# Attention with 192-wide heads beside a gated feed-forward, on one core: the last 64 value channels split by key parity instead of by query halves, and the vector engine's side work placed differently

## The chip, the core and the metric

The kernel runs on one core of a Trainium2 chip. The metric is the device time of one execution in microseconds; runs are compared by their median.

## The reference, cut to what matters

```python
def _A_ref(x, k_cache, v_cache, wq, wo):        # x: 1 x 2048 x 640, caches: 1 x 32 x 2048 x 192
    q = (x @ wq).reshape(B, Sq, H, Dh).transpose(0, 2, 1, 3)
    scores = einsum("bhqd,bhkd->bhqk", q, k_cache) * (Dh ** -0.5)
    p = softmax(scores, axis=-1)
    o = einsum("bhqk,bhkd->bhqd", p, v_cache)
    return o.transpose(0, 2, 1, 3).reshape(B, Sq, H * Dh) @ wo
def _B_ref(x, w1, w3, w2):                      # 640 -> 1536 -> 640
    return (silu(x @ w1) * (x @ w3)) @ w2
xn = layernorm(A_x)
return A_x + _A_ref(xn, ...) * silu(_B_ref(xn, ...))
```

Everything is bf16 in memory. There are 32 heads (H), each with 2048 queries and 2048 keys.

## The kernel before

**Tiling.** The work goes head by head (`h`), in each head by four query blocks of 512 (`qb`), and in each block by eight steps (`p`). A step handles 256 keys: keys lie on 128 partitions, and a second index (`t` or `u`, 0 for even and 1 for odd keys) holds the two keys of a partition. `scores` writes 128 keys x 1024 (even and odd keys, 512 queries each) into one PSUM tile `st2`; `weights` takes the exponential of it on ScalarE into `pT2` (line 558); `values` or `values_quads` multiplies `pT2` by the values `vt` and accumulates over the eight steps into two PSUM tiles, `obank` (`acc["o"]`), of two banks each.

**Quads.** Heads 2 to 30 (`in_quads`) run TensorE as four 64 x 64 arrays. Two of them share an output half (column halves, `c`), two share the rows of the contraction (`r`); the two row halves write to different tiles `acc["o"][0]` and `acc["o"][1]`, which are added at the end. `values_quads` (line 629) has three parts per step: `high(0)` and `high(1)` make the first 128 of 192 channels from even and odd keys, four matmuls of 512 queries each; `low` makes the last 64 channels. Before the change the column halves of `low` hold the two halves of the queries: four matmuls of 256 queries for the even keys and four for the odd keys. Its 256 columns fill half of the second bank of each tile.

**End of a block.** `evict_quads` runs after the last `low` of a block: a ScalarE copy of the first tile to SBUF (`oa`, line 653), a VectorE addition of the second tile (`ot`, line 654), and a DMA transpose into `ox` (line 655). The tiles `obank` are single, so the next block's first `values` matmuls wait for both. All instructions named here are pinned to the order in which the program writes them. `step` writes, at `p == 1` of the next block, first what is left of the old block with `evict_quads`, then the exponential of step 1, and then `project_chunk`: 40 matmuls (line 355) that make the next head's queries, into a tile of the same pool as the scores. That pool (`ps_st`, tag `st2`) has two buffers A and B. Step 0's scores use A, step 1's B, the projection A, step 2's B again. So step 2's scores wait for step 1's exponential, and ScalarE makes that one behind the copy `oa`.

**Row sums.** The sums of the softmax are made on VectorE from `pT2` (`row_sums`): `fours` adds two `pT2` tiles, `join`, `fold` and `ends` (line 662) bring a block to 512 columns, and a DMA transpose turns the result (`eT`, line 688). `turned_sums` reduces it, takes the reciprocal `rl`, and writes the scaled outputs into `ostage` (lines 702 to 709). These steps are put off by a number of steps with `later` and are run by `do_chores` when the step counter has come so far. `pT2` has three buffers, so an exponential three tiles on waits for `fours`. In the last head (`h == H - 1`) `do_chores` does nothing at the first two steps of a block.

**Bound steps.** What the next head needs for its softmax shift (maxima over the keys, column lengths of the query weights, `head_bound`) stands in a list `lazy`; `do_chores` takes one entry at certain steps of a block (`slots`): steps 5, 6 and 7 in even heads and head 1, step 5 in the other odd heads.

After the heads come the rest of the feed-forward and the output projection.

Of the kernel before, what the change touches and what calls it, by code (L numbers as in the profile page):

```python
# [10 lines left out]
ALU = mybir.AluOpType  # L11
AX = mybir.AxisListType
BF16 = mybir.dt.bfloat16
F32 = mybir.dt.float32
I32 = mybir.dt.int32

P = 128
DH = 192
DT = DH - P
# [11 lines left out]
def _kernel_impl(ctx, tc, A_x, A_k_cache, A_v_cache, A_wq, A_wo, B_w1, B_w3, B_w2, out):  # L31
    nc = tc.nc
    _, SQ, D = A_x.shape
    _, H, SK, dh = A_k_cache.shape
# [5 lines left out]
    NQB = SQ // 512  # L40
    NKT = SK // P
    NPAIR = NKT // 2
# [11 lines left out]
    ROWS = (slice(0, DT), slice(DT, P))  # L54
# [21 lines left out]
    pin = tc.keep_in_program_order  # L76
# [73 lines left out]
    def in_quads(h):  # L150
        return 1 < h < H - 1
# [14 lines left out]
    with ExitStack() as actx:  # L166
# [27 lines left out]
        sums = lnx.tile([P, len(ASUM)], F32, name="sums")  # L194
# [122 lines left out]
        acc = {}  # L317
# [245 lines left out]
        def stage(h, qb):  # L563
            if (h // HG, qb) not in stages:
                stages[h // HG, qb] = [stp.tile([P, 4, HG * DH], BF16, tag=f"ostage{qb}", name="ostage"), HG]
            return stages[h // HG, qb][0]

        def staged(h, qb):
            stages[h // HG, qb][1] -= 1
            if stages[h // HG, qb][1] == 0:  # L570
                g0 = h - h % HG
                keep = pin if in_quads(h) else (lambda x: x)
                acc["store"] = keep(nc.sync.dma_start(
                    out=o_scr[qb].rearrange("(t p) c -> p t c", p=P)[:, :, g0 * DH:(g0 + HG) * DH],
                    in_=stages.pop((h // HG, qb))[0][:, :, :]))
# [46 lines left out]
        def values_quads(hd, qb, p, pT2):  # L622
            vt = hd["L"]["vt"]

            def sums(t, low):
                for c in range(2):
                    c0, q0, n = (P, c * 256, 256) if low else (c * DT, 0, 512)
                    for r in range(2):
                        pin(nc.tensor.matmul(acc["o"][r][ROWS[c], int(low), 0:n], lhsT=vt[ROWS[r], t, p, c0:c0 + DT],  # L629
                                             rhs=pT2[ROWS[r], t * 512 + q0:t * 512 + q0 + n],  # L630
                                             start=(p == 0 and t == 0), stop=(p == NPAIR - 1 and t == 1)))

            def high(t):
                if p == 0 and t == 0:
                    acc["o"] = [ps_o.tile([P, 2, 512], F32, tag=f"ob{b}", name=f"obank{b}") for b in range(2)]
                sums(t, False)

            def low():
                sums(0, True)
                sums(1, True)  # L640
                if p == NPAIR - 1:
                    evict_quads(hd, qb, [ob[:].rearrange("p t c -> p (t c)")[:, 0:768] for ob in acc["o"]])

            fs = [lambda: high(0), low, lambda: high(1)]
            if p in (0, NPAIR - 1):
                fs = [fs[0], fs[2], fs[1]]
            return [((hd["h"], qb), f) for f in fs]

        def evict_quads(hd, qb, banks):
            oa = aq["one"].tile([P, 768], F32, tag="oa", name="oa")  # L650
            ot = aq["two"].tile([P, 768], BF16, tag="ot", name="ot")
            ox = aq["two"].tile([P, 6, P], BF16, tag="ox", name="ox")
            pin(nc.scalar.copy(out=oa[:], in_=banks[0]))  # L653
            pin(nc.vector.tensor_tensor(out=ot[:], in0=oa[:], in1=banks[1], op=ALU.add))  # L654
            pin(nc.sync.dma_start_transpose(out=ox[:], in_=ot[:]))
            hd["ox"][qb] = ox

        def later(wait, f, *a):
            chores.append((clock[0] + wait, f, a))

        def add(out, a, b):
            pin(nc.vector.tensor_tensor(out=out, in0=a, in1=b, op=ALU.add))  # L662

        def row_sums(hd, qb, p, w):
            sm = hd["sums"]

            def fours():
                t = aq["tree"].tile([P, 2, 1024], BF16, tag="tree", name="tree")
                a, b = sm["w"]
                sm["w"] = []  # L670
                add(t[:], a[:], b[:])
                sm["t"].append(t)

            def join():
                a, b = sm["t"]
                add(a[:], a[:], b[:])
                sm["t"].pop()

            def fold():
                t = sm["t"][0]  # L680
                add(t[:, 0, :], t[:, 0, :], t[:, 1, :])

            def ends():
                t = sm["t"].pop()[:, 0, :]
                e = aq["two"].tile([P, 512], BF16, tag="e", name="e")
                add(e[:], t[:, 0:512], t[:, 512:1024])
                eT = aq["two"].tile([P, 4, P], BF16, tag="eT", name="eT")
                pin(nc.sync.dma_start_transpose(out=eT[:], in_=e[:]))
                later(6, turned_sums, hd, qb, eT)

            sm["w"].append(w)
            if p % 4 == 3:
                later(2, fours)
            if p == NPAIR - 1:
                for f in (join, fold, ends):
                    later(4, f)

        def turned_sums(hd, qb, eT):
            h, hg = hd["h"], hd["h"] % HG
            ox = hd["ox"].pop(qb)  # L700
            rs = stt.tile([P, 4], F32, tag="rs", name="rs")
            pin(nc.vector.tensor_reduce(out=rs[:], in_=eT[:], axis=AX.X, op=ALU.add))
            rl = rl_all[:, h * NQT + qb * 4:h * NQT + qb * 4 + 4]
            pin(nc.vector.reciprocal(out=rl, in_=rs[:]))
            o0 = hg * DH

            pin(nc.vector.tensor_tensor(out=stage(h, qb)[:, :, o0:o0 + P], in0=ox[:, 0:4, :],
                                        in1=rl.unsqueeze(2).to_broadcast([P, 4, P]), op=ALU.mult))
            pin(nc.vector.tensor_tensor(out=stage(h, qb)[:, :, o0 + P:o0 + DH].rearrange("p (c j) d -> p c j d", c=2),
                                        in0=ox[:, 4:6, :].rearrange("p j (c d) -> p c j d", c=2),  # L710
                                        in1=rl.rearrange("p (c j) -> p c j", c=2).unsqueeze(3).to_broadcast([P, 2, 2, DT]),
                                        op=ALU.mult))
            staged(h, qb)

        clock = [0]
# [2 lines left out]
        aq = {}  # L718

        def do_chores(h, qb, p):  # L720
            if h == H - 1 and p < 2:
                return
            for c in [c for c in chores if c[0] <= clock[0]]:
                chores.remove(c)
                c[1](*c[2])
            slots = (5, 6, 7) if h % 2 == 0 or h == 1 else (5,)
            if p in slots and lazy and lazy[0][0] <= clock[0]:
                _, f, a = lazy.pop(0)
                f(*a)
# [15 lines left out]
        def step(hd, qb, p, extra=None):  # L745
            me = (hd["h"], qb)
            first = qb == 0 and p < 2
            st2 = scores(hd, qb, p, quads=before["quads"] if first else hd["quads"])
            old = [k for k, _ in parts if k != me]
            old_quads = bool(old) and heads_quads(old[0][0])  # L750
            if p == 1 and old_quads:
                while parts[0][0] != me:
                    next_part()
            pT2 = weights(st2, hd["nb"][qb], p)
            parts.extend((values_quads if hd["quads"] else values)(hd, qb, p, pT2))
            if hd["quads"] and p % 2 == 1:
                row_sums(hd, qb, p, acc["w"])
            if p == 0:
                while sum(k != me for k, _ in parts) > (2 if old_quads else 1):
                    next_part()  # L760
            elif p == 1:
                while parts[0][0] != me:
                    next_part()
            else:
                while len(parts) > (4 + (p > 2) if hd["quads"] else 3):
                    next_part()
            if extra:
                extra()
            while late:
                late.pop(0)()  # L770
            clock[0] += 1
            do_chores(hd["h"], qb, p)
# [129 lines left out]
        hx = fw.tile([P, SQ], BF16, name="hx")  # L902
        astack = ExitStack()
        fdp = astack.enter_context(tc.tile_pool(name="fdp", bufs=1, side="right"))
        for name, n in (("one", 1), ("two", 2), ("tree", 3)):
            aq[name] = astack.enter_context(tc.tile_pool(name=f"aq_{name}", bufs=n, side="right"))
        ffn_w_loads = [
            lambda: pin(nc.gpsimd.dma_start(out=w1_sb[:], in_=B_w1[:, FPIG + P:F].rearrange("(c p) f -> p c f", p=P))),
# [57 lines left out]
        for h in range(1, H):  # L966
# [10 lines left out]
            hd = heads[h]  # L977
# [420 lines left out]
```

## Time and profile before

| | us |
|---|---|
| median of 3 runs | 1926.5 (1925.24 to 1927.55) |
| the profiled execution, its own time | 1925.79 |
| its span | 1924.3 |
| TensorE (PE) busy | 1914.5 (99%) |
| VectorE (DVE) busy | 1446.4 (75%) |
| ScalarE (ACT) busy | 1350.4 (70%) |
| GpSimd (POOL) busy | 600.3 (31%) |

The heads end at about 1636 us of the span; the feed-forward and the output projection follow, and there VectorE and ScalarE have little to do. In a profile line, L558 is line 558 of the kernel; "out<-in" names the tiles; "x116" is a count; PEld are weight loads, which run beside the matmuls; SPq is the queue of SyncE, which starts DMAs. In the timeline a row begins with its start and its length in us, and a bracket at its end says how long the engine had been idle before, and what ended that.

### The profile page before, as it was taken

Reading aid. Unit: us, or ns where it says so; the run is one execution under the profiler, and the core shown is the slowest. Engines: PE = TensorE matmul, PEld = TensorE weight load, DVE = VectorE, ACT = ScalarE, POOL = GpSimd, SP = SyncE. Lnnn points to the kernel's source line nnn. Section 1 sums busy time; section 2 is a strip of 40 time slices with the busy share of each in tenths; the row PEclk is TensorE's granted clock in tenths of the full one; section 3 lists DMA queues with packets and bytes.
Section 4 is the critical chain, followed back from the end, with each engine's and each line's share of the span. In section 5 each row is a group of like instructions: output and inputs, shape, how many; then the busy total and the mean of one; then the engine's idle time right before and its main releaser. Section 6 shows DMA issues by size and latency. Waiting matters only on the chain.

```text
span 1924.3 us, 75788 instructions
## 1 busy us (share of the span) xinstructions
PE 1914.5 (99%) x34631; PEld 1306.8 (68%) x34631; DVE 1446.4 (75%) x2326; ACT 1350.4 (70%) x1405; POOL 600.3 (31%) x757
## 2 busy tenths in 40 slices
PE   9999999999999999999999999999999999999999
PEld 5666667777777777777777777777777796454446
DVE  8668888888888888988888888888888875521111
ACT  7778888888888888888888888888888877210000
POOL 3433434343434333344333343433343320000000
PEclk9999999999999999999999999999999999999999
DMA  7714446444553455345544453446444523936763
GB/s 171 142 50 74 106 84 102 86 100 87 93 98 86 99 84 100 81 105 91 101 84 104 76 107 68 112 77 110 77 106 85 97 45 119 281 71 152 162 151 76
DMA packets 535684, 197.22 MB, mean 102 GB/s; under 512 B 486896, under 2 KB 528848, under 8 KB 535360
## 3 DMA queue, kind: packets, MB, share of 16 engines
q1 hardware_dynamic: 522416, 162.71, 43.5%
q0 software_dynamic: 8256, 24.58, 4.9%
q8 instruction: 271, 4.44, 1.0%
q10 hardware_dynamic: 4688, 5.05, 0.8%
q14 instruction: 53, 0.43, 0.1%
HBM read 54.26 MB, written 31.98 MB: 45 GB/s over the span
## 4 chain that ended last, share of the span: by engine, by line
PE 99%; SPq 0%; DVE 0%; ACT 0%; DMA 0%; POOL 0%; issue 0%; ACTq 0%
PE st L550 34%; PE obank L629 31%; PE ps L355 14%; PE ps_s L1142 8%; PE obank L609 3%; PE ps_s L1098 3%; PE ps_f L1162 2%; PE ps_gu L929 1%; PE ps_f L1178 1%; PE ps L340 0%; DMA KT<-in_A_k_cache_dram 0%; SPq L116 0%; PE ps_gu L340 0%; ACT pT L558 0%; SPq L100 0%; ACT xnT L283 0%
## 5 line engine op out<-in xcount | busy, mean ns | idle before, releaser
L558 ACT ACTIVATE pT<-st,nb 128x1024 bf16<-128x1024 f32 x1016 | 1124.6, 1113 | 182.0 <-PE st L550 151.6
L629 PE MATMUL obank<-pT,vt 64*64 64x256 bf16 (+1 forms) x14848 | 787.8, 323 | 0.0
L629 PEld LDWEIGHTS <-vt 64*64 64x64 bf16 x14848 | 499.7, 107 | 172.4 <-issue 1.9
L550 PE MATMUL st<-qS,KM 64*64 64x512 bf16 (+1 forms) x1951 | 416.7, 376 | 0.4 <-POOL qS L381 0.4
L550 PE MATMUL st<-qA,KT 64*64 64x512 bf16 (+1 forms) x1951 | 416.6, 376 | 0.0
L550 PE MATMUL st<-qD,KT 64*64 64x512 bf16 (+1 forms) x1951 | 416.6, 376 | 0.0
L550 PE MATMUL st<-qA,KM 64*64 64x512 bf16 (+1 forms) x1951 | 392.0, 376 | 0.0
L550 PE MATMUL st<-qS,KT 64*64 64x512 bf16 (+1 forms) x1951 | 391.9, 376 | 0.1
L550 PE MATMUL st<-qF,KT 64*64 64x512 bf16 (+1 forms) x1951 | 391.8, 376 | 0.0
L550 PEld LDWEIGHTS <-KT 64*64 64x64 bf16 (+1 forms) x7808 | 286.6, 107 | 129.8 <-issue 0.6
L381 POOL COPY qS<-qA 64x512 bf16<-64x512 bf16 x256 | 291.0, 1137 | 63.9 <-DVE qA L378 28.2
L662 DVE TENSOR_TENSOR tree<-pT,pT 128x2048 bf16<-128x2048 bf16 x232 | 299.7, 1292 | 1.6 <-ACT pT L558 1.6
L355 PE MATMUL ps<-xnT,wq 64*64 64x512 bf16 (+1 forms) x2390 | 291.8, 376 | 0.0
L355 PE MATMUL ps<-xnS,wq 64*64 64x512 bf16 (+1 forms) x2390 | 288.0, 376 | 0.0
L662 DVE TENSOR_TENSOR tree<-tree 128x2048 bf16<-128x2048 bf16 x232 | 265.8, 1146 | 4.0
L355 PEld LDWEIGHTS <-wq 64*64 64x64 bf16 (+1 forms) x4780 | 170.2, 107 | 74.7
L550 PEld LDWEIGHTS <-KM 64*64 64x64 bf16 (+1 forms) x3904 | 152.0, 106 | 54.8 <-issue 1.2
L385 POOL COPY qD<-qF 64x512 bf16<-64x512 bf16 x127 | 95.6, 753 | 292.1 <-ACT qF L378 288.2
L1142 PE MATMUL ps_s<-oT,wo_sb 128*128 128x512 bf16 x720 | 155.7, 379 | 0.0
L378 DVE CAST qA<-ps 128x512 bf16<-128x512 f32 x120 | 82.9, 691 | 95.2 <-ACT qF L378 94.6
L654 DVE TENSOR_TENSOR ot<-oa,obank 128x768 bf16<-128x768 f32 x116 | 110.1, 949 | 36.2 <-ACT oa L653 35.8
L653 ACT COPY oa<-obank 128x768 f32<-128x768 f32 x116 | 92.6, 798 | 62.8 <-PE obank L629 62.8
(159 smaller groups left out, 1628.8 us busy)
## 6 DMA issues: line engine op xcount, KB each, us to landing
o_scr<-ostage SPq DMA_DIRECT2D x64, 384.0 KB, 3.2
vt<-in_A_v_cache_dram SPq DMA_DIRECT2D x62, 384.0 KB, 4.9
wo_sb<-in_A_wo_dram POOLq DMA_DIRECT2D x1, 7680.0 KB, 30.6
wq<-in_A_wq_dram POOLq DMA_DIRECT2D x31, 160.0 KB, 4.2
hT_scr<-hblk SPq DMA_DIRECT2D x16, 256.0 KB, 2.9
xnS<-xnT POOLq DMA_DIRECT2D x8, 320.0 KB, 6.1
wq<-in_B_w_dram POOLq DMA_DIRECT2D x31, 80.0 KB, 3.7
wq<-in_A_wq_dram POOLq DMA_DIRECT2D x31, 80.0 KB, 3.3
```

Of the source, the lines that this page charges most:

```text
L355: pin(nc.tensor.matmul(halves[t][c, :], lhsT=w[ROWS[t], s, c], rhs=xs[ROWS[t], s // 2, qs], start=(s == 0), stop=(s == 2 * DC - 1)))
L378: pin(c(out=dst[:, qs], in_=src))
L381: keep(nc.gpsimd.tensor_copy(out=qS[ROWS[t], qs], in_=qA[ROWS[1 - t], qs]))
L385: keep(copy(out=qD[:, qs], in_=qF[PGW:P, qs]))
L550: pin(nc.tensor.matmul(st2[c, t * 512:(t + 1) * 512], lhsT=k[:, c], rhs=q[ROWS[t], qs], start=(s == 0), stop=(s == 2)))
L558: pin(nc.scalar.activation(out=pT2, in_=st2[:], func=ACT.Exp, scale=SCALE, bias=nb[:]))
L609: pin(nc.tensor.matmul(acc["o"][b][:, r, (j % 2) * 256:(j % 2) * 256 + DH + 1], lhsT=pT2[ROWS[r], t * 512 + j * P:t * 512 + (j + 1) * P], ...
L629: pin(nc.tensor.matmul(acc["o"][r][ROWS[c], int(low), 0:n], lhsT=vt[ROWS[r], t, p, c0:c0 + DT], rhs=pT2[ROWS[r], t * 512 + q0:t * 512 + q0 ...
L653: pin(nc.scalar.copy(out=oa[:], in_=banks[0]))
L654: pin(nc.vector.tensor_tensor(out=ot[:], in0=oa[:], in1=banks[1], op=ALU.add))
L662: pin(nc.vector.tensor_tensor(out=out, in0=a, in1=b, op=ALU.add))
L1142: pin(nc.tensor.matmul(ps_of[d], lhsT=wo_sb[:, k, d * P:(d + 1) * P], rhs=part(k // KQ)[:, k % KQ, :], start=(k == 0), stop=(k == OC - 1)))
```

## The change

The last 64 channels: the column halves of `low` now hold the key parities. Column half 0 takes the even keys and half 1 the odd keys, each for all 512 queries, so `low` is four matmuls of 512 per step in place of eight of 256. The second bank of each tile is filled whole, and `oa`, `ot` and `ox` grow from 768 to 1024 columns. After the transpose the two parities lie beside each other in `ox`; `turned_sums` adds them (64 + 64 columns for each of four query tiles), and then scales.

The side work: the last head no longer skips `do_chores` at the first two steps; the last `turned_sums` of head 30 is put off by 9 steps instead of 6; in even heads the blocks 0 and 2 use the steps 5 and 6 for `lazy`, the blocks 1 and 3 still 5, 6 and 7. The pool of the `tree` tiles has two buffers instead of three.

```diff
             def sums(t, low):
                 for c in range(2):
-                    c0, q0, n = (P, c * 256, 256) if low else (c * DT, 0, 512)
+                    c0, u = (P, c) if low else (c * DT, t)
                     for r in range(2):
-                        pin(nc.tensor.matmul(acc["o"][r][ROWS[c], int(low), 0:n], lhsT=vt[ROWS[r], t, p, c0:c0 + DT],
-                                             rhs=pT2[ROWS[r], t * 512 + q0:t * 512 + q0 + n],
-                                             start=(p == 0 and t == 0), stop=(p == NPAIR - 1 and t == 1)))
+                        pin(nc.tensor.matmul(acc["o"][r][ROWS[c], int(low), :], lhsT=vt[ROWS[r], u, p, c0:c0 + DT],
+                                             rhs=pT2[ROWS[r], u * 512:(u + 1) * 512],
+                                             start=(p == 0 and (low or t == 0)), stop=(p == NPAIR - 1 and (low or t == 1))))
...
             def low():
                 sums(0, True)
-                sums(1, True)
                 if p == NPAIR - 1:
-                    evict_quads(hd, qb, [ob[:].rearrange("p t c -> p (t c)")[:, 0:768] for ob in acc["o"]])
+                    evict_quads(hd, qb, [ob[:].rearrange("p t c -> p (t c)")[:] for ob in acc["o"]])
...
         def evict_quads(hd, qb, banks):
-            oa = aq["one"].tile([P, 768], F32, tag="oa", name="oa")
-            ot = aq["two"].tile([P, 768], BF16, tag="ot", name="ot")
-            ox = aq["two"].tile([P, 6, P], BF16, tag="ox", name="ox")
+            oa = aq["one"].tile([P, 1024], F32, tag="oa", name="oa")
+            ot = aq["two"].tile([P, 1024], BF16, tag="ot", name="ot")
+            ox = aq["two"].tile([P, 8, P], BF16, tag="ox", name="ox")
...
-                later(6, turned_sums, hd, qb, eT)
+                later(6 if in_quads(hd["h"] + 1) or qb < NQB - 1 else 9, turned_sums, hd, qb, eT)
...
-            pin(nc.vector.tensor_tensor(out=stage(h, qb)[:, :, o0 + P:o0 + DH].rearrange("p (c j) d -> p c j d", c=2),
-                                        in0=ox[:, 4:6, :].rearrange("p j (c d) -> p c j d", c=2),
-                                        in1=rl.rearrange("p (c j) -> p c j", c=2).unsqueeze(3).to_broadcast([P, 2, 2, DT]),
-                                        op=ALU.mult))
+            low = ox[:, 4:8, 0:DT]
+            pin(nc.vector.tensor_tensor(out=low, in0=low, in1=ox[:, 4:8, DT:P], op=ALU.add))
+            pin(nc.vector.tensor_tensor(out=stage(h, qb)[:, :, o0 + P:o0 + DH], in0=low,
+                                        in1=rl.unsqueeze(2).to_broadcast([P, 4, DT]), op=ALU.mult))
...
         def do_chores(h, qb, p):
-            if h == H - 1 and p < 2:
-                return
             for c in [c for c in chores if c[0] <= clock[0]]:
                 chores.remove(c)
                 c[1](*c[2])
-            slots = (5, 6, 7) if h % 2 == 0 or h == 1 else (5,)
+            slots = (5,) if h % 2 and h > 1 else (5, 6) if h > 1 and qb % 2 == 0 else (5, 6, 7)
...
-        for name, n in (("one", 1), ("two", 2), ("tree", 3)):
+        for name, n in (("one", 1), ("two", 2), ("tree", 2)):
```

## The prediction, made before the changed kernel was run

> **What bounds the kernel now.** I read the page first (busy times, then the chain that ended last), then the groups kept apart by shape, then the chain and the timeline of one query block.
>
> ```profile
> span 1924.3 us, 75788 instructions
> PE 1914.5 (99%) x34631; PEld 1306.8 (68%) x34631; DVE 1446.4 (75%) x2326; ACT 1350.4 (70%) x1405; POOL 600.3 (31%) x757
> PE 99%; SPq 0%; DVE 0%; ACT 0%; DMA 0%; POOL 0%; issue 0%; ACTq 0%
> ...
> L629 PE MATMUL obank<-pT,vt 64*64 64x512 bf16 x7424 | 608.0, 376 | 0.0
> L629 PE MATMUL obank<-pT,vt 64*64 64x256 bf16 x7424 | 385.7, 269 | 0.0
> L654 DVE TENSOR_TENSOR ot<-oa,obank 128x768 bf16<-128x768 f32 x116 | 110.1, 949 | 36.2 <-ACT oa L653 35.8
> L653 ACT COPY oa<-obank 128x768 f32<-128x768 f32 x116 | 92.6, 798 | 62.8 <-PE obank L629 62.8
> L558 ACT ACTIVATE pT<-st,nb 128x1024 bf16<-128x1024 f32 x1016 | 1124.6, 1113 | 182.0 <-PE st L550 151.6 <-DVE km L466 4.2 <-DVE tree L662 3.7
> ```
>
> TensorE carries the whole chain and is hardly ever idle. So only two things count: what the change saves TensorE, and every wait that it puts in front of TensorE, in full, since TensorE has no slack to catch up with. There are 116 quad blocks (the count of `oa`), with eight steps each, 928 steps.
>
> **TensorE's own work.** The chain of one block in order of time:
>
> ```profile
> 803.39 0.43 PE obank L629 x12
> 803.82 2.16 PE ps L355 x40
> 805.98 0.65 PE st L550 x12
> ...
> 809.44 0.65 PE obank L629 x16
> 810.09 0.65 PE st L550 x12
> ```
>
> A step of values has 16 matmuls before: eight of 512 columns and eight of 256. It takes 0.65 us, as long as the 12 score matmuls of 512. Spread over four arrays, both stream 3 x 512 columns, so eight matmuls of 256 cost what four of 512 cost, within the 0.01 us of the row. A finer bound comes from the block. By the next part's windows it repeats every 12.54 us, and it holds 48 + 10 = 58 groups of four matmuls of 512 (or two of 256); the projection shows 2.16 / 10 = 0.216 us for a group. 58 x 0.216 = 12.53, which leaves 0.01 us for eight `low` parts, 1 to 3 ns each with the rounding. I take 2 ns x 928 = **-2 us** (from 0 to -4.6, the 0.005 us by which the rows can be off).
>
> The Trainium skill ("TensorE: Matmul & The Clock Gate", "Wait — 56ns, not 53.3ns?") states a fixed cost of about 2.5 ns per warm matmul. With one matmul fewer on each array per step that gives -2.3 us, an estimate from the page; the trace agrees as far as it resolves.
>
> **The wider copy, and what stands behind it.** The start of a block, from the timeline, the windows of five blocks and one place where step 2's scores did wait:
>
> ```profile
> 803.86 0.80 ACT L653 COPY oa<-obank 128x768 f32<-128x768 f32 x1 [0.55 <-PE obank L629]
> 804.56 1.12 ACT L558 ACTIVATE pT<-st,nb 128x1024 bf16<-128x1024 f32 x1
> 805.78 0.38 PE L550 MATMUL st<-qS,KM 64*64 64x512 bf16 x1
> 805.81 0.38 PE L550 MATMUL st<-qA,KM 64*64 64x512 bf16 x1
> ...
> 1544.92 1.12 ACT L558 ACTIVATE pT<-st,nb 128x1024 bf16<-128x1024 f32 x1
> 1546.09 0.37 PE L550 MATMUL st<-qS,KM 64*64 64x512 bf16 x1
> ...
> 841.70:854.24 12.54, 12.54 (x269) 9.06 (x265) 11.59 (x24) 10.19 (x10) 3.11 (x3) 1.00 0.53 123
> 879.44:891.98 12.54, 12.54 (x269) 9.07 (x265) 11.92 (x17) 10.50 (x11) 3.28 (x4) 1.00 0.27 29
> ...
> L378 ACT CAST qF<-ps 128x512 bf16<-128x512 f32 x123 | 72.0, 586 | 41.9 <-PE ps L355 41.9
> ```
>
> ScalarE is 70% busy, but not at this place. The copy `oa` starts when the old block's last `low` is done (803.86). Step 1's exponential stands behind it in program order and ends at 804.56 + 1.12 = 805.68. Step 2's scores need its PSUM buffer, and TensorE, coming out of the projection, is there at 805.78. At 1546 the first array was early and really waited: 1544.92 + 1.12 = 1546.04 to 1546.09, so the release takes 0.05 us. The cover is therefore 0.05 us on the first array, and 0.08 on the other three, which come at 805.81.
>
> The copy grows by 256 columns. From 512 to 768 columns ScalarE's copies go from 586 to 798 ns, 0.83 ns per column, so +0.21 us. The exponential then ends at 805.89, TensorE is released at 805.94, and the three later arrays lose 805.94 - 805.81 = 0.13 us (the first loses 0.16, of which 0.03 only uses up its lead). The projection cannot cover more: it is already done. The end of the last `low` is no earlier either, since the same columns are streamed. Of 116 blocks the last runs its step 2 in head 31, where this was not the last wait; 115 x 0.13 = **+15 us**. Bounds: 0.10 per block if the release is a little faster (+11.5); 0.23 if the copy of 1024 took as long as the exponential of 1024, 1113 ns (+26).
>
> **VectorE.** `ot` grows too: from the cast of 512 f32 columns (691 ns, below) to 768 (949) it is 1.0 ns per column, +0.26 us. `turned_sums` gets one addition of 128x256, and its last multiplication keeps its size.
>
> ```profile
> L378 DVE CAST qA<-ps 128x512 bf16<-128x512 f32 x120 | 82.9, 691 | 95.2 <-ACT qF L378 94.6
> L709 DVE TENSOR_TENSOR ostage<-ox,rl_all 128x256 bf16<-128x256 bf16 x116 | 48.4, 418 | 0.0
> 810.50 0.43 DVE L662 TENSOR_TENSOR e<-tree 128x512 bf16<-128x512 bf16 x1
> ...
> 778.95 1.22 DVE L662 TENSOR_TENSOR tree<-pT,pT 128x2048 bf16<-128x2048 bf16 x1
> 780.09 0.95 DVE L654 TENSOR_TENSOR ot<-oa,obank 128x768 bf16<-128x768 f32 x1
> 781.35 0.41 PE L629 MATMUL obank<-pT,vt 64*64 64x512 bf16 x4
> ```
>
> The addition is not in the trace. Between half of the 0.43 of a 512-wide addition and the 0.42 of the same size, with about 0.1 us more because the multiplication now depends on it, it is 0.3 to 0.45 us. Queued behind it are `fours` and then `ot`, and TensorE's next values wait for `ot`. In most blocks `ot` waits for `oa` (idle before it: 35.8 us over the group) and ends 0.7 us or more before TensorE needs it, so 0.21 + 0.26 fit. Not so where the queue is full. At block 3 of an even head (head 14 above, where steps 5, 6 and 7 still hold bound work) `ot` ends at 781.04. Then +0.56 to +0.71 and 0.05 for the release give 781.65 to 781.80, against 781.38 for the second tile's matmuls plus the 0.13 above, 781.51. That is 0.15 to 0.3 us in 14 even heads, **+3 us**. Blocks 0 of even heads, as full before, lose a key maximum at step 7 and gain room. It goes to block 1 with its two GpSimd copies, the column lengths follow one place later, and the head's bound with its GpSimd reduction moves one place on in block 2; the next head needs that five or more steps later, so I cost these moves at nothing, and at one late exponential per even head if the cover fails. None of them carries a DMA with it. Range 0 to +9 (0.6 us per even head, one more block late in each).
>
> The DMA transpose of `ox` carries a third more; its data are used a block later, so I cost it at nothing. If that cover failed, a late transpose would push `turned_sums`, `fours` and `ot` by its lateness. The `tree` tiles with two buffers cost nothing: writers and readers are all on VectorE, in order.
>
> **The last head.** Around 1586 us TensorE has its one long wait among the heads:
>
> ```profile
> ACT pT L558 <- DVE tree L662: 3.7, 1, 3.7
> PE obank L609 <- ACT pT L558: 2.9, 1, 2.9
> 1582.67 0.95 DVE L654 TENSOR_TENSOR ot<-oa,obank 128x768 bf16<-128x768 f32 x1 [5.86 <-ACT oa L653]
> 1585.21 0.68 DVE L702 TENSOR_REDUCE rs<-eT 128x4 f32<-128x512 bf16 x1
> 1587.08 1.22 DVE L662 TENSOR_TENSOR tree<-pT,pT 128x2048 bf16<-128x2048 bf16 x1
> 1588.41 2.12 ACT L558 ACTIVATE pT<-st,nb 128x1024 bf16<-128x1024 f32 x2 [3.73 <-DVE tree L662]
> ```
>
> The exponential needs a `pT` buffer that `fours` still reads, and `fours` waits at step 2 because the last head skips its chores. VectorE was idle for 5.86 us just before. Without the skip, `rs` to `fours` run in that hole and the wait goes: **-2.9 us**. What is late next is the scores themselves, which TensorE paces. If `rs` waits for its DMA there, 1 us may come back. Head 30's last `turned_sums`, put off by three steps, writes only into `ostage`; its store goes out with head 31, so nothing waits for it.
>
> **Sum.** -2 + 15 + 3 - 2.9 = +13.1 us on the profiled execution's own 1925.79 (span 1924.3 and 1.5 around it), 1938.9. The median of the runs lies 0.7 higher, 1926.5, so I predict **1939.6 us**. A difference within 0.2% (3.9 us) is about what a measurement of this kernel cannot tell from none.
>
> **The rivals.**
> *The exponential's end stays hidden* (ends not slower). Place: step 2's scores of each block. It decides at a growth of 0.05 to 0.08 us of the copy: if the copy grew no more, only -2 - 2.9 + 3 remain, 1924.6. Against it: 586 to 798 ns for 256 columns, and the same 12.54 us in blocks 38 us apart, so the cover has no room elsewhere. 0.07.
> *A matmul has a large fixed cost* (ends faster). If each of the 256-wide matmuls carried some 25 ns that a wider one would not repeat, one fewer per array and step is 928 x 25 = 23 us: 1939.6 + 2 - 23 = 1918.6. Against it: the equal 0.65 us of 16 and 12 matmuls above. The Trainium skill ("TensorEngine Tiling (Array Packing)", "Instruction Overhead") speaks of about 60 cycles for each matmul, which would be this case; the trace does not show it at 256 columns. 0.03.
> *VectorE becomes the bound.* The fuller of the two windows above has VectorE busy for 11.92 of 12.54 us; with 0.26 + 0.4 it would be 12.58. If `ot` comes 0.2 us late in half of all blocks, 58 x 0.2 = 11.6 us instead of 3: 1948; more with slower additions, 1955. For it: the full blocks; against: the window before has 11.59, and most have idle time before `ot`. 0.10.
>
> **How the numbers follow.** The forecast has the remaining 0.80; its terms at their ends give 11.5 - 4.6 - 2.9 + 0 = +4 and 26 - 0 - 1.9 + 9 = +33. All terms at their upper ends together are unlikely; I take +4 to +27, 1930 to 1953, which also holds the lower part of the VectorE case. Slower by over 0.2%: 0.80 and 0.10, less 0.04 for a forecast whose terms all come out low, 0.86. Within 0.2%: the hidden case less a little that falls lower, and that 0.04, 0.08. Faster: 0.06.
>
> **What would show it.** Right: `oa` near 1.01 us; step 2's scores starting 0.05 us after the exponential behind `oa`; a block period of about 12.65 us (12.54 + 0.13 - 0.02); the line-609 wait of 2.9 us gone; `ot` late only after block 3 of even heads. Wrong: a block period still at 12.54 or below, or values steps below 0.64 us, or `ot` late in many blocks.

## The result, and the profile after

The changed kernel takes 1939.27 us (median of 6 runs, 1939.19 to 1940.69), the kernel before 1927.2 us (6 runs, 1925.24 to 1927.98). The ratio is 1.0066, with a 95% interval of 1.0056 to 1.0076: slower by 0.7%, a small loss, but clear of the spread of the runs. The span of the profiled execution grew from 1924.3 to 1937.6 us.

The page of the changed kernel:

```profile
span 1937.6 us, 68457 instructions
PE 1929.3 (100%) x30896; PEld 1266.1 (65%) x30919; DVE 1510.7 (78%) x2442; ACT 1375.1 (71%) x1405; POOL 592.1 (31%) x757
PE 97%; DVE 1%; DMA 1%; SPq 0%; ACT 0%; issue 0%; POOL 0%
```

and its groups by shape:

```profile
L629 PE MATMUL obank<-pT,vt 64*64 64x512 bf16 x11136 | 794.2, 376 | 0.3 <-DVE ot L653 0.2
L653 DVE TENSOR_TENSOR ot<-oa,obank 128x1024 bf16<-128x1024 f32 x116 | 141.3, 1218 | 36.4 <-ACT oa L652 35.6
L652 ACT COPY oa<-obank 128x1024 f32<-128x1024 f32 x116 | 117.4, 1012 | 62.2 <-PE obank L629 62.2
L709 DVE TENSOR_TENSOR ox<-ox 128x256 bf16<-128x256 bf16 x116 | 32.9, 283 | 0.0
```

TensorE has 3712 matmuls fewer: its weight loads went from 34631 to 30919, and 23 of the matmuls are missing from this trace. It is still the chain, but now VectorE and a DMA hold 1% of it each. The copy takes 1012 ns instead of 798, the addition 1218 instead of 949, and there is a new addition of 283 ns.

A page that says "PE 100% busy" hides the loss: a matmul's row lasts 0.38 us, but the next group of four starts 0.22 us behind it, so rows overlap and a late one only starts late. It is seen in the chain of one block in order of time (start, length, what):

```profile
811.00 2.16 PE ps L355 x40
813.16 0.80 PE st L550 x12
813.96 1.08 PE obank L629 x20
815.04 0.65 PE st L550 x12
```

The 12 score matmuls behind the projection take 0.80 us, where they took 0.65 in the kernel before; the next 12, at 815.04, take 0.65 again. The timeline shows why (start, length, engine, line, operation):

```profile
811.04 1.01 ACT L652 COPY oa<-obank 128x1024 f32<-128x1024 f32 x1 [0.54 <-PE obank L629]
811.95 1.12 ACT L558 ACTIVATE pT<-st,nb 128x1024 bf16<-128x1024 f32 x1
...
813.12 0.37 PE L550 MATMUL st<-qS,KM 64*64 64x512 bf16 x1
813.12 0.40 PE L550 MATMUL st<-qA,KM 64*64 64x512 bf16 x1
813.13 0.40 PE L550 MATMUL st<-qS,KM 64*64 64x512 bf16 x1
813.13 0.40 PE L550 MATMUL st<-qA,KM 64*64 64x512 bf16 x1
813.33 0.37 PE L550 MATMUL st<-qA,KT 64*64 64x512 bf16 x1
813.36 0.38 PE L550 MATMUL st<-qS,KT 64*64 64x512 bf16 x1
```

The exponential ends at 811.95 + 1.12 = 813.07, and the scores start 0.05 us later. Groups of four matmuls are 0.216 us apart; this one starts 0.372 us after the last group of the projection.

At the last head, the view of waits between 1592 and 1620 us, where the wait of 2.9 us would now be:

```profile
ACT pT L558 <- PE st L550: 3.8, 9, 1.0
DVE osum L581 <- PE obank L609: 3.0, 1, 3.0
DVE rs L701 <- DMA eT<-e: 2.4, 1, 2.4
```

No TensorE wait is left there, and the exponential no longer waits for VectorE.

**Where the 13.3 us are.** Read from the trace as the time from one projection's first matmul to the next, the median block takes 12.672 us, before 12.538. With 115 blocks that is +15.4 us. Blocks over the median cost 1.2 us more than before, the stretch from the last quad block to the feed-forward fell from 51.73 to 48.64 us (-3.1), and the feed-forward and output projection are the same (286.65 us from the start of their first to that of their last matmul in both).

The term of the last head rests on one profile of the kernel before, and its time, 1925.79 us, lies below the median of 1927.2. The five other profiled kernels that keep the skip (among the runs below) spend 53.2 to 53.6 us in this stretch. With 53.3 in place of 51.73 the term is -4.7, and the sum +11.9, which is what lies between the two medians (12.1).

### The profile page after: what moved, and what is told of

It reads as the page before. It is cut to its first block, busy times and chain, and to the rows that moved or that the text cites. A ratio compares the mean times of both kernels' runs of the same rounds, so it can differ in the third digit from the quotient of the medians.

```text
span 1937.6 us, 68457 instructions
## 1 busy us (share of the span) xinstructions
PE 1929.3 (100%) x30896; PEld 1266.1 (65%) x30919; DVE 1510.7 (78%) x2442; ACT 1375.1 (71%) x1405; POOL 592.1 (31%) x757
## 4 chain that ended last, share of the span: by engine, by line
PE 97%; DVE 1%; DMA 1%; SPq 0%; ACT 0%; issue 0%; POOL 0%
PE st L550 34%; PE obank L629 31%; PE ps L355 14%; PE ps_s L1139 8%; PE obank L609 3%; PE ps_s L1095 3%; PE ps_f L1159 2%; PE ps_gu L926 1%; PE ps_f L1175 1%; DMA eT<-e 0%; DVE tree L661 0%; PE ps L340 0%; DMA KT<-in_A_k_cache_dram 0%; SPq L116 0%; DVE ot L653 0%
## 5 line engine op out<-in xcount | busy, mean ns | idle before, releaser
L629 PE MATMUL obank<-pT,vt 64*64 64x512 bf16 x11136 | 794.2, 376 | 0.3 <-DVE ot L653 0.2
L629 PEld LDWEIGHTS <-vt 64*64 64x64 bf16 x11136 | 430.7, 107 | 193.1 <-issue 3.7
L550 PE MATMUL st<-qS,KM 64*64 64x512 bf16 (+1 forms) x1951 | 423.8, 377 | 0.3 <-POOL qS L381 0.3
L550 PE MATMUL st<-qD,KT 64*64 64x512 bf16 (+1 forms) x1951 | 424.0, 376 | 0.0
L550 PE MATMUL st<-qA,KT 64*64 64x512 bf16 (+1 forms) x1951 | 423.9, 376 | 0.0
L550 PEld LDWEIGHTS <-KT 64*64 64x64 bf16 (+1 forms) x7808 | 297.1, 106 | 128.3 <-issue 0.6
L355 PEld LDWEIGHTS <-wq 64*64 64x64 bf16 (+1 forms) x4780 | 182.5, 107 | 83.2
L653 DVE TENSOR_TENSOR ot<-oa,obank 128x1024 bf16<-128x1024 f32 x116 | 141.3, 1218 | 36.4 <-ACT oa L652 35.6
L652 ACT COPY oa<-obank 128x1024 f32<-128x1024 f32 x116 | 117.4, 1012 | 62.2 <-PE obank L629 62.2
L1139 PEld LDWEIGHTS <-wo_sb 128*128 128x128 bf16 x720 | 70.4, 98 | 84.9 <-issue 0.2
```

What stands on the lines that cost most here:

```text
L355: pin(nc.tensor.matmul(halves[t][c, :], lhsT=w[ROWS[t], s, c], rhs=xs[ROWS[t], s // 2, qs], start=(s == 0), stop=(s == 2 * DC - 1)))
L550: pin(nc.tensor.matmul(st2[c, t * 512:(t + 1) * 512], lhsT=k[:, c], rhs=q[ROWS[t], qs], start=(s == 0), stop=(s == 2)))
L629: pin(nc.tensor.matmul(acc["o"][r][ROWS[c], int(low), :], lhsT=vt[ROWS[r], u, p, c0:c0 + DT], rhs=pT2[ROWS[r], u * 512:(u + 1) * 512], sta ...
L1139: pin(nc.tensor.matmul(ps_of[d], lhsT=wo_sb[:, k, d * P:(d + 1) * P], rhs=part(k // KQ)[:, k % KQ, :], start=(k == 0), stop=(k == OC - 1)))
```

## The experiments

The theory: ScalarE's wider copy holds up the exponential, and that holds up TensorE. The rivals: VectorE's added work, or the matmuls themselves. Ratios are against the kernel before, run on the same chip.

**The matmuls alone.** The four 512-wide matmuls, with the old eviction of 768 columns; the last 64 channels of this kernel's output are therefore incomplete.

```diff
# in the kernel before
-                    c0, q0, n = (P, c * 256, 256) if low else (c * DT, 0, 512)
+                    c0, u = (P, c) if low else (c * DT, t)
...
                 sums(0, True)
-                sums(1, True)
```

> The kernel before with the changed matmuls alone: four of 512 columns in the low part, while the copy, the addition and the transpose still take 768 columns. The odd keys' share of the last 64 channels is left out of the output. If the loss sits in the wider copy, this kernel has none of it and gains only what eight matmuls of 256 cost more than four of 512: 2 us, so about 0.999 of the kernel before. If a matmul carried a large fixed cost, some 25 ns on each array and step, it would be 23 us faster (0.988). If the new matmuls themselves cost the 13 us, it is as slow as the changed kernel (1.007).

Measured: 1925.57 us, ratio 0.9993 (0.9984 to 1.0002). The interval reaches 1, so the gain is not shown by the times; the trace resolves it. The median block takes 12.518 us, 0.020 less than before, 2.3 us over 115 blocks. (It is 12.538 or 12.539 in all four profiles with the old matmuls and no added delay.) A `low` part is 2 to 3 ns shorter. The 23 us of a large fixed cost and a loss in the matmuls are both excluded. That the span shrank only by 0.3 us comes from the last head, whose stretch (53.34 us) was 1.6 us longer than in the profile before, as in the other kernels that keep the skip; its reason was not followed.

**A delay behind the copy, in three sizes.** One more ScalarE instruction between `oa` and the exponential, everything else as before, but for the `tree` pool, which has two buffers as in the changed kernel. The first try read `oa` itself:

```diff
             pin(nc.scalar.copy(out=oa[:], in_=banks[0]))
+            oj = aq["one"].tile([P, 185], BF16, tag="oj", name="oj")
+            pin(nc.scalar.copy(out=oj[:], in_=oa[:, 0:185]))
```

> The kernel before with one more ScalarE instruction behind the copy oa: a copy of 185 columns from SBUF to a tile that nobody reads, made to delay the exponential by the 0.21 us by which the wider copy delays it. Matmuls, VectorE's work, transposes and the skip are as before. Theory (the exponential behind the copy): step 2's scores start 0.15 us later in each of 115 blocks, +15 to +18 us, ratio 1.008 to 1.009. Rival (VectorE's added work makes the loss): nothing changes, 1.000.

Measured: 1961.22 us, 1.0179 (1.0165 to 1.0193), twice what was expected. The dose was wrong: the extra copy started only when `oa` was complete (807.22 + 0.80 = 808.02), and the exponential came 0.39 us late:

```profile
807.22 0.80 ACT L653 COPY oa<-obank 128x768 f32<-128x768 f32 x1 [0.55 <-PE obank L629]
808.05 0.35 ACT L655 CAST oj<-oa 128x185 bf16<-128x185 f32 x1
```

In the other two runs it reads a tile that has long been ready (`in_=xnT[:, 0, 0:185]`, then `0:4`).

> The kernel before with one more ScalarE instruction behind oa, a copy of 185 columns from a tile that has long been ready, so that it waits for nothing: the exponential comes 0.21 us later, as in the changed kernel, and nothing else changes. Theory: +0.15 us in 115 blocks, +17.5 us, ratio 1.009. If only the last three arrays count, +0.13 and +15 us, 1.008. Rival (VectorE's added work): 1.000.

Measured: 1947.26 us, 1.0108 (1.0093 to 1.0123), above the theory's 1.009: the delay came to 0.248 us instead of 0.21. Here the extra copy starts before `oa` ends (813.29 + 0.80 = 814.09):

```profile
813.29 0.80 ACT L653 COPY oa<-obank 128x768 f32<-128x768 f32 x1 [0.55 <-PE obank L629]
813.99 0.35 ACT L655 COPY oj<-xnT 128x185 bf16<-128x185 bf16 x1
```

> The small dose: the kernel before with a copy of 4 columns behind oa, from a tile that has long been ready. By the run with 185 columns, whose exponential came 0.245 us later, at 0.83 ns per column the delay is 0.245 - 0.150 = 0.095 us. Theory (cover of 0.057 us, then one for one): 0.038 us per block, 115 blocks, +4.4 us, ratio 1.0023, period 12.576 us. Rival (the delay counts from nothing): 0.095 x 115 = +11 us, 1.0057. Rival (any further instruction at this place costs a fixed time): as with 185 columns, 1.0108.

Measured: 1930.59 us, 1.0019 (1.001 to 1.0028). The block of the small dose, from its timeline:

```profile
804.94 0.80 ACT L653 COPY oa<-obank 128x768 f32<-128x768 f32 x1 [0.55 <-PE obank L629]
805.64 0.20 ACT L655 COPY oj<-xnT 128x4 bf16<-128x4 bf16 x1
805.74 1.12 ACT L558 ACTIVATE pT<-st,nb 128x1024 bf16<-128x1024 f32 x1
```

and its chain:

```profile
804.91 2.16 PE ps L355 x40
807.06 0.68 PE st L550 x12
```

The scores behind the projection take 0.68 us, 0.03 over the undisturbed 0.65. All four delays lie close to one line. The delay is the exponential's start behind `oa`'s, less the 0.695 us of the kernel before; the growth is that of the median block (for the changed kernel against 12.518, its own matmuls without the delay):

| kernel | delay, us | growth of a block, us | difference |
|---|---|---|---|
| pad of 4 columns | 0.096 | 0.036 | 0.060 |
| changed kernel | 0.213 | 0.154 | 0.059 |
| pad of 185, ready tile | 0.248 | 0.187 | 0.061 |
| pad of 185, from `oa` | 0.388 | 0.317 | 0.071 |

So there is a cover of 0.06 us (0.07 at the largest dose), and beyond it TensorE loses one for one. Neither rival moved in these runs: matmuls, additions and transposes are those of the kernel before.

**VectorE's work alone.** One more addition behind `ot` that reads the second accumulator, and the new 128x256 addition; the results go nowhere.

```diff
             pin(nc.vector.tensor_tensor(out=ot[:], in0=oa[:], in1=banks[1], op=ALU.add))
+            oj = aq["one"].tile([P, 192], BF16, tag="oj", name="oj")
+            pin(nc.vector.tensor_tensor(out=oj[:], in0=oa[:, 0:192], in1=banks[1][:, 0:192], op=ALU.add))
...
+            oy = aq["one"].tile([P, 4, DT], BF16, tag="oy", name="oy")
+            pin(nc.vector.tensor_tensor(out=oy[:], in0=ox[:, 0:4, 0:DT], in1=ox[:, 0:4, DT:P], op=ALU.add))
```

> The kernel before with VectorE's added work alone: behind ot one more addition of 192 columns that reads the second accumulator (so that the tile is released as late as by the wider ot, plus the start of an instruction), and the 128x256 addition in front of the last multiplication. ScalarE, matmuls and transposes are as before; the added results go nowhere. Theory (the copy): a few late additions, 0 to +5 us, ratio 1.000 to 1.003. Rival (VectorE): +13 us or more, 1.007.

Measured: 1933.17 us, 1.0031 (1.0019 to 1.0042), some 6 us: a little more than the theory's 0 to 5, and half of what the rival needs. The median block stays at 12.539; the loss lies in single blocks, which cost 6.2 us over the median, where the kernel before has 1.0. The timeline behind block 3 of head 14:

```profile
782.28 0.95 DVE L654 TENSOR_TENSOR ot<-oa,obank 128x768 bf16<-128x768 f32 x1
783.14 0.35 DVE L656 TENSOR_TENSOR oj<-oa,obank 128x192 bf16<-128x192 f32 x1
```

and the chain there:

```profile
782.91 0.65 PE st L550 x12
783.56 1.15 PE obank L629 x18
```

The scores behind the projection are undisturbed at 0.65 us, but the values wait for the late addition. From the starts of the second tile's matmuls these waits come to 0.10 us on average behind the blocks 0 and 0.11 us behind the blocks 3 of even heads, 4.0 us in all. In the changed kernel the same sum over all blocks is 1.6 us, although its VectorE work is as large (1511 us busy, here 1498): its scores are already 0.15 us late, which gives the addition that time, and its slots are spread. Two losses at one place do not add.

**The old slots for the bound steps**, in the changed kernel:

```diff
-            slots = (5,) if h % 2 and h > 1 else (5, 6) if h > 1 and qb % 2 == 0 else (5, 6, 7)
+            slots = (5, 6, 7) if h % 2 == 0 or h == 1 else (5,)
```

> The changed kernel with the bound steps where they were, at the steps 5, 6 and 7 of every block of an even head. Theory: the blocks 0 of even heads have a key maximum at step 7 again, and their addition ends 0.1 to 0.3 us too late in 15 blocks: +1.5 to +4.5 us against the changed kernel, 1.0075 to 1.009. Rival (the spread does nothing): as the changed kernel, 1.0066.

Measured: 1939.68 us, 1.0067 (1.0053 to 1.008), not to be told from the changed kernel's 1.0066. Behind the blocks 0 of even heads the additions were not late; over all blocks these waits came to 2.4 instead of 1.6 us in the traces. My theory of 0.1 to 0.3 us in 15 blocks was wrong: with undisturbed scores, in the run before this one, the additions there came some 0.15 us late in ten of the 15 heads, and the scores' delay of 0.15 us covers that.

**The last head.** First the skip alone, taken out of the kernel before:

```diff
         def do_chores(h, qb, p):
-            if h == H - 1 and p < 2:
-                return
```

> The kernel before, in which only the last head no longer skips its put-off work at the first two steps. Theory: TensorE's wait of 2.9 us at the start of the last head goes, -3.0 us, ratio 0.9985. Rival: the wait comes back as one for the transpose or for VectorE, 1.000.

Measured: 1924.26 us, 0.9988 (0.9979 to 0.9997), the span 1.7 us shorter, the median 2.9. Part of the gain came back in a new place. A TensorE wait between 1575 and 1600 us:

```profile
PE obank L609 <- DVE osum L582: 1.0, 1, 1.0
```

and VectorE's timeline there:

```profile
1595.65 0.68 DVE L702 TENSOR_REDUCE rs<-eT 128x4 f32<-128x512 bf16 x1
1596.36 0.18 DVE L704 RECIPROCAL rl_all<-rs 128x4 f32<-128x4 f32 x1
1596.57 0.69 DVE L707 TENSOR_TENSOR ostage<-ox,rl_all 128x512 bf16<-128x512 bf16 x1
1597.18 0.42 DVE L709 TENSOR_TENSOR ostage<-ox,rl_all 128x256 bf16<-128x256 bf16 x1
1597.51 0.55 DVE L581 COPY osum<-obank 128x386 f32<-128x386 f32 x1
```

Head 30's `turned_sums` now stands right in front of the last head's own eviction `osum`, which TensorE waits for. The change's other edit, 9 steps instead of 6, moves it away:

```diff
-                later(6, turned_sums, hd, qb, eT)
+                later(6 if in_quads(hd["h"] + 1) or qb < NQB - 1 else 9, turned_sums, hd, qb, eT)
```

> The kernel before without the skip in the last head, as in the earlier run of that edit, and with the last turned_sums of head 30 put off by 9 steps. The earlier run gained 1.7 us of span and showed a new wait of 1.0 us of TensorE for the last head's own eviction. Theory: putting the row sums off takes them out of that eviction's way, and the whole 3.0 us of the changed kernel's tail appear: span 1921.3, ratio 0.9985. Rival: the 9 steps do nothing, span 1922.6.

Measured: 1922.53 us, 0.9978 (0.9969 to 0.9987), span 1921.2. The stretch from the last quad block to the feed-forward is 48.68 us, as in the changed kernel. Both edits together are worth the 3 us between the profiles. Between the medians it is 4.5 us (1927.0 to 1922.53), in keeping with a stretch of 53.3 us where the skip is kept.

**A way around the copy.** If the loss is the copy's, copying the first half while TensorE makes the last low part should remove it. First in place, within the same PSUM tiles:

```diff
             def low():
+                if p == NPAIR - 1:
+                    acc["oa"] = aq["one"].tile([P, 1024], F32, tag="oa", name="oa")
+                    pin(nc.scalar.copy(out=acc["oa"][:, 0:512], in_=acc["o"][0][:, 0, :]))
                 sums(0, True)
...
-            pin(nc.scalar.copy(out=oa[:], in_=banks[0]))
+            pin(nc.scalar.copy(out=oa[:, 512:1024], in_=banks[0][:, 512:1024]))
```

> The changed kernel with the copy oa in two instructions: the first 512 columns are written before the block's last low part, so that ScalarE copies them while TensorE makes the low part; the other 512 follow. Theory: two copies of 512 take 0.49 us each until the next instruction, and the first starts 0.22 us earlier, so the exponential comes only about 0.06 us later than in the kernel before, which its cover holds; the changed kernel's loss of about 17 us goes and its gains stay: about 1922 us, ratio 0.997 to 0.998. Rival (VectorE): the additions still come as late and the loss stays at 1.005 or more, or moves to the wait for the addition.

Measured: 2020.32 us, 1.0485 (1.0471 to 1.05): far off. TensorE's longest wait in this kernel, from the view of waits:

```profile
PE obank L629 <- ACT oa L641: 78.3, 116, 0.7
```

and the chain at one block:

```profile
807.60 0.23 PE obank L629 x3
807.83 0.02 issue
807.86 0.59 ACT oa L641
808.45 0.04 issue
808.49 0.41 PE obank L629 x4
```

The low matmuls write the other bank of the tile that the copy reads, and still the low part waits for the copy, 116 times 0.7 us: the two are ordered by tile, as the next version confirms, where the wait is gone. The run says nothing on the theory. The second version gives the first 128 channels of both row halves one PSUM tile and the last 64 channels the other, and copies and adds each half on its own:

```diff
-                        pin(nc.tensor.matmul(acc["o"][r][ROWS[c], int(low), :], lhsT=vt[ROWS[r], u, p, c0:c0 + DT],
+                        pin(nc.tensor.matmul(acc["o"][int(low)][ROWS[c], r, :], lhsT=vt[ROWS[r], u, p, c0:c0 + DT],
...
             def low():
+                if p == NPAIR - 1:
+                    acc["ot"] = aq["two"].tile([P, 1024], BF16, tag="ot", name="ot")
+                    evict_half(0)
                 sums(0, True)
                 if p == NPAIR - 1:
+                    evict_half(1)
...
+        def evict_half(k):
+            oa = aq["one"].tile([P, 512], F32, tag=f"oa{k}", name="oa")
+            pin(nc.scalar.copy(out=oa[:], in_=acc["o"][k][:, 0, :]))
+            pin(nc.vector.tensor_tensor(out=acc["ot"][:, k * 512:(k + 1) * 512], in0=oa[:], in1=acc["o"][k][:, 1, :], op=ALU.add))
```

> The changed kernel with the accumulators laid out by channel group: one PSUM tile holds the first 128 channels of both row halves, the other the last 64, so that copying the first no longer makes the low matmuls wait. The first 512 columns are copied and added while the last low part runs, the other 512 behind it. Theory: the exponential behind the copies comes 0.06 us later than in the kernel before, about as much as its cover; the changed kernel's 0.15 us per block and most waits for the addition go: block period 12.52 us, about 1920 to 1922 us, ratio 0.996 to 0.9975. Rival (VectorE carries the loss): with one more instruction per block on VectorE it stays at 1.005 or more.

Measured: 1922.99 us, 0.9982 (0.9973 to 0.9991), a little short of the theory's 0.9975. Its timeline:

```profile
803.33 1.07 ACT L654 COPY oa<-obank 128x512 f32<-128x512 f32 x2 [0.34 <-PE obank L629]
804.29 1.13 ACT L558 ACTIVATE pT<-st,nb 128x1024 bf16<-128x1024 f32 x1
```

and its chain:

```profile
803.50 2.16 PE ps L355 x40
805.66 0.65 PE st L550 x12
```

The same 1024 columns are copied, VectorE has one instruction more than in the changed kernel, and the scores take 0.65 us again. The block takes 12.524 us, 0.006 over the kernel with the matmuls alone. This repairs the change, 16 us below it. The split also brings the addition forward, so this run alone takes away both causes; the delays above are what tells them apart. It does not beat the kernel before with the two edits of the last head alone (1922.53); the two cannot be told apart, so of the change only the last head's edits are shown to gain in the time of a run; the matmuls' 2.3 us stand in the trace alone.

## Why the prediction was right, step by step

It gave 1939.6 us, and 1939.27 was measured. The mechanism was the one it named, but that the total fits to 0.3 us is luck: the copy was put 2.7 us too low, and VectorE 1.8 us too high.

- *The matmuls*: -2 predicted, 0.020 us x 115 = -2.3 in the trace of the matmuls alone. The equal rows of 16 and 12 matmuls were read rightly. This is also the estimate that the prediction worked out from the Trainium skill's fixed cost per warm matmul ("TensorE: Matmul & The Clock Gate", "Wait — 56ns, not 53.3ns?"); the trace agrees. The overhead of some 60 cycles for each matmul that the Trainium skill also states ("TensorEngine Tiling (Array Packing)", "Instruction Overhead") would have given far more; the trace does not show it at 256 columns.
- *The copy*: the step from 798 to 1010 ns was right (1012), and so was the release (0.05 us). The term was mis-sized: +15 predicted, 0.154 x 115 = +17.7 measured. The failed step is "the three later arrays lose 0.13, the first loses 0.16, of which 0.03 only uses up its lead". In the timeline after, all four arrays start within 0.01 us at 813.12, but in the next group the first leads by 0.03 again (813.33 against 813.36): the lead is not a reserve, the others fall behind at once, and a block loses what the first array loses (within 0.003 us in all four delayed kernels).
- *VectorE*: +3 predicted; the blocks over the median cost 1.2 us more than before. The place was half wrong. "`ot` late only after block 3 of even heads": the waits there averaged 0.01 us, those behind the blocks 3 of odd heads 0.035, and two large ones (0.4 and 0.5 us) came behind block 2 of heads 16 and 28. The price of the added instruction was right: 0.283 us, and 0.32 until the next one starts, in a range of 0.3 to 0.45.
- *The transpose*, costed at nothing: not quite. In the chain before the large wait at head 16 stands a DMA transpose, that of `eT`, with the row sums and the addition behind it:

```profile
868.81 4.38 DMA eT<-e
...
875.41 1.22 DVE tree L661
876.63 1.14 DVE ot L653
877.81 1.24 PE obank L629 x17
```

  The longer `ox` transpose is not needed for this: with VectorE's work alone, where `ox` is as before, the same chain stands in front of the largest late addition (0.4 us, behind block 2 of head 6):

```profile
359.25 4.37 DMA eT<-e
...
365.80 1.14 DVE tree L664
366.94 0.86 DVE ot L654
```

  So VectorE's longer queue behind a late `eT` is enough; why `eT` takes 4.4 us there, where the median is 2.5 us in the changed kernel and 3.1 us in this one, stays open.
- *The last head*: -2.9 predicted, -3.1 measured in its stretch between the two profiles, and about -4.7 against the other kernels with the skip. I gave the whole credit to the skip; the runs show that 1.5 us of it (stretches of 50.16 and 48.68 us without and with them) depend on the 9 steps, which I had costed at nothing.
- *Rivals.* The hidden exponential and the large fixed cost are excluded by the doses and by the matmuls alone. VectorE as the bound did not come: its work alone cost 6 us, and in the changed kernel the waits for its addition come to 1.6 us.

## What to carry to other kernels

An engine with 30% idle time can still stand in front of the bound at one place of the loop: measure the time there, from the end of its instruction to the start of the waiting matmul, less the release, and hold every added column against it. Here that was 0.06 us, and a delay of 0.21 us cost 0.15 us 115 times over. When two added costs meet at the same wait, do not add them up; and when an accumulator is to be drained in parts, put the parts into tiles of their own.

## What was not expected of the hardware

The four 64 x 64 arrays do not run in step, and their offset is not fixed. In the kernel before, the first array starts the scores behind the projection 0.03 us ahead of the others in 102 of 115 blocks, but 0.003 us ahead in the first ten and 0.065 us in the last three; it changed twice, both times behind a wait. With VectorE's work alone the lead is 0.08 to 0.09 us in most blocks. In the changed kernel, where all four start together behind each projection (0.003 to 0.010 us apart), a lead of 0.03 us is back in the next group (0.028 to 0.035). So there a wait costs the delay of the array that leads, not that of the arrays that come later.

A ScalarE copy that reads what the copy before it wrote starts only when that one is done (0.03 us behind its end, where a copy from a ready tile starts 0.10 us ahead of it): 185 columns put 0.39 us in front of the exponential when they came from `oa`, and 0.25 us when they came from a tile that was ready.
